# Two tiles' rows turned on TensorE in attention's last slot, and routing's steps moved by one place

## The chip, the cores and the metric

The kernel runs on one core of a Trainium2 chip. The metric is device time in microseconds (us) of one execution, the median of three runs. Engines are named as in the profile: PE is TensorE (PEld its weight load), DVE is VectorE, ACT is ScalarE, POOL is GpSimd, SP is SyncE, which here only issues DMAs.

## The reference

Inputs are q, k, v of shape (8, 8, 576, 64) (batch, heads, positions, head size), a gate matrix of 512x8, a local gate of 512x1, and for each of eight experts w1 (512x1024) and w2 (1024x512). What is computed, cut to what matters:

```python
scores = scale * np.matmul(q, k.transpose(0, 1, 3, 2))
scores = np.where(block_i >= block_j, scores, -1000000000.0)   # blocks of 64 positions
attn = np.exp(scores - max) / sum
x = np.matmul(attn, v)      # as (8, 576, 512)
...
logits = x @ w_gate
local_gate = 1.0 / (1.0 + np.exp(-(x @ w_local)))
for b in range(B):
    prev_e = -1
    for s in range(S):
        fresh_e = int(np.argmax(logits[b, s]))
        e = fresh_e if s == 0 or local_gate[b, s] < 0.5 else prev_e
        prev_e = e
        p = softmax(logits[b, s])
        out[b, s] = p[e] * (np.maximum(x[b, s] @ w1[e], 0.0) @ w2[e])
```

So each row of x goes to one expert, and which one may depend on the row before it in the same batch.

## The kernel before, in words

**Attention** runs in 32 slots, one for each pair of heads of a batch (loop at L1184; four slots make a batch). A slot i holds, in the order of the code: `behind(i)` (the values of pair i-1 on PE, L1007; sums and logits of a half batch, L705, with a copy on ACT, L714; four additions on DVE, L1019, in `add_chunks`), then the scores of pair i (L971 to L973) with the exponentials on ACT (L983, L995), then the transposes for pair i+1 (`kq`, L692, copied to `qkT` by ACT, L945), then `turns_of(i)` (x of an earlier batch is turned to rows by PE, `trx`, scaled by DVE, L818, and stored).

**Routing** is a generator of steps (`tokens`, L304 to L399; the class `Steps`, L16 to L59). A step ends in a `yield` of its kind: "V" for DVE alone, "T" or "PE" where the next step begins with a product on PE. The code of the slots calls for steps at fixed places, `steps.tensor()` for one that begins on PE, `steps.all()` for all that are left. Four steps of a group of batches begin on PE: `rta` (L329, a transpose; DVE reads it at L331 to L336), `rtb` (L339; read at L343 to L346), `rtd` (L349; read at L351, and L352 to L356 make the one-hot `oh` from it) and `rtr` (L362, L363: counts of `oh`; copied by DVE at L365 and L367). Then DVE goes on alone (L370 to L394), and the factors p[e] are stored by SP (L399, which the trace shows as L673 or L677). The third group (ten blocks of 128 rows) has its turn in slots 30 and 31, the last batch's later, between the expert tiles.

**The banks.** These products write to PSUM tiles of two banks, which `bank_of` (L894) gives out: a second taker gets the other half of the same tile, except that a name that begins with "rt" always begins a fresh tile. Waits go by tile: who writes into one half waits for readers of the other.

**Expert tiles.** Rows of one expert are gathered (POOL, L651) into tiles of 128 (`xgs`). A tile needs its rows with the 512 values on the partitions (`xT`), the expert's w1 as bf16 in a contiguous buffer (a DVE copy of 128x4096: L1071 for the first two tiles, L1337 for those that follow), the first products (`first_mm`, 32 on PE, L1086; ReLU on ACT, L1089), the second (`second_mm`, 8 on PE, L1283; scaled by ACT, L1291) and an indirect store by POOL (L1294). The expert of a tile is known only at run time: its number is loaded into registers of PE and DVE (L1095).

The rows of the first four tiles (`AHEAD`) are turned by four DMA transposes on SP's queue at the end of slot 30 (L1253), into `free`, a part of an attention buffer that is no longer used (shown as S); later tiles' rows by DMA transposes from the tile loop (L1350). The first tile's weights go to Pc of even pairs, after slot 31's `behind`; the second's to `qkT`, after pair 31's values; the third's to `w1c`, a buffer at the place of `qkT`.

**Handing over**, in the order of the code: slot 31; POOL's drain (L1261); values of pair 31 (L1007); a routing step that begins on PE (`rtr`); the second tile's weights (L1071); the last `add_chunks` (L1019); `steps.all()` (L1268: routing's L370 to L394); the first tile's products; the last half batch's gates (L705); then the tile loop, whose turn i brings weights of tile i+1, first products of tile i, steps of the last batch's routing (`point()`), gathers and second products of tile i-1. In turn i = 1 stand the second tile's first products. Steps of the last batch that the prediction speaks of: L705 to L710, the logits (`trl` on PE, L728; DVE at L737 to L753) and its own `tokens` (L312 to L394), with rows turned at L720.

Of the kernel before, what the change touches and what calls it, by code (L numbers as in the profile page):

```python
# [62 lines left out]
def kernel(  # L63
# [11 lines left out]
    nc = tc.nc  # L75
# [753 lines left out]
    with tc.tile_pool(name="atn_const", bufs=1) as cst, \  # L829
# [63 lines left out]

        def bank_of(nm):  # L894

            if not half or nm.startswith("rt"):
                half.clear()
                ps = psp.tile([P, 2, 512], F32, tag="sc", name=nm)
                half.extend([ps[:, 1], ps[:, 0]])
            return half.pop()  # L900
# [2 lines left out]
            half.clear()  # L903
            return psp.tile([P, 2, 512], F32, tag="sc", name=nm)

        half = []
        banks["of"], banks["both"] = bank_of, banks_of
        po = psp.tile([P, 1024], F32, tag="o", name="o", bufs=1)

# [121 lines left out]
        def turns_of(i):  # L1031

            b, r = divmod(i, HP)
            if r == 1 and b:
                return [lambda: logits_of(b - 1)]
            if r == 2 and b:
                return [lambda: rows_of_batch(b - 1, (0, 1)), lambda: rows_of_batch(b - 1, (4,))]
            if r == 3 and b:
                return [lambda: rows_of_batch(b - 1, (2, 3))]
            return []  # L1040

        T1 = scratch_of_weights(0)

# [102 lines left out]
        def run(tasks):  # L1146
            for task in tasks:
                half.clear()
                task()()
# [34 lines left out]
        for i in range(NPAIR):  # L1184
            slot[0] = i
            load_qk(i + 2)


            swap = i == 1
            if not swap:  # L1190
                behind(i)
            if i == NPAIR - 1:

                tiles = [(0, j) for j in range(NS[0])] + [(1, j) for j in range(NS[1])]
                ev = {j: expert(*tiles[j]) for j in range(2)}
                w = weights_at(bf(Pc[0], WE), ev[0])
            soon = 2 < i < NPAIR - 1 and i % 2
            if soon:
                last_scores(i)
            for u in range(len(UNITS)):  # L1200
                ps = scores(i, u)
                if u < 2 or i < 2:
                    exps(i, u, ps)
                if u == 0:
                    if not soon:
                        last_scores(i)
                    if i == 0:
                        transposes(1, 8)
                        constants()
                        for h in range(2):  # L1210
                            hs = slice(64 * h, 64 * h + 64)
                            nc.sync.dma_start(
                                out=wg2[hs, :, 16 * h:16 * h + E],
                                in_=moe_w_gate.rearrange("(p h d) e -> h d p e", h=2, d=D)[h])
                            nc.sync.dma_start(
                                out=wg2[hs, :, 16 * h + E:16 * h + E + 1],
                                in_=moe_w_local.rearrange("(p h d) e -> h d p e", h=2, d=D)[h])
            if swap:
                behind(i)
            last = lambda: exps(i, 2, ps) if i > 1 else None  # L1220
            if i == NPAIR - 2:
                last()
                last = lambda: None
                run([lambda: half_batch(B - 1, 0)])
            if i:
                transposes(i + 1, 6 if swap else 0,
                           last)
            if swap:
                add_chunks(i - 1)
            if i == NPAIR - 1:  # L1230
                routing(i)
            run(turns_of(i))
            slot[0] = i + 0.5
            if i % HP == 0 or NPAIR - 3 <= i < NPAIR - 1:
                routing(i)
            if i < NPAIR - 1:
                vector(END[i % HP])
            arrange(i + 2, [nc.gpsimd.tensor_copy] * 2)
            while pending:
                pending.pop(0)()  # L1240

            if wload < 2 * E - 2 and i == 2 + 2 * wload:
                load_weights(*divmod(wload, 2))
                wload += 1
            if i < NPAIR - 1:
                release(queue=nc.gpsimd)
            if i == NPAIR - 2:

                free = bf(Sb[(NPAIR - 3) % NSB], 2 * S * 2)[:, -AHEAD * Dm:]
                xTs = {}  # L1250
                for j in range(AHEAD):
                    xTs[j] = free[:, j * Dm:(j + 1) * Dm].rearrange("p (k n) -> p k n", k=KO1)
                    nc.sync.dma_start(out=xTs[j], in_=row_of_x(xgs[j]), transpose=True)  # L1253
                load_weights(E - 1, 1)
        assert not pending
        slot[0] = NPAIR
# [8 lines left out]
        steps.tensor()  # L1265
        w_next = weights_at(qkT.rearrange("p j a s -> p (j a s)").bitcast(BF16)[:, :WE], ev[1])
        add_chunks(NPAIR - 1)
        steps.all()  # L1268

        hT = op.tile([P, S], F32, tag="oT", name="hT", bufs=HP + 3)  # L1270
        prev = first_mm(xTs.pop(0), w, hT.bitcast(BF16)[:, :FO * P].rearrange("p (k n) -> p k n", k=FO),
# [3 lines left out]
    with tc.tile_pool(name="ffn_s", bufs=2, reuse_waits="tile") as f_p, \  # L1275
# [77 lines left out]

        def gathers(last, behind=None):
            while nx[0] <= min(last, len(tiles) - 1):
                if tiles[nx[0]] == (1, 0) and (chain.next, others.next) != ("end", "end"):
                    if nx[0] > i + 2:
                        break
                    others.all()
                    chain.all()  # L1360
                    release()
                gather(*tiles[nx[0]], behind=behind)

# [28 lines left out]
        for i, (ph, j) in enumerate(tiles):  # L1392
            now, done = w, prev
            waiting = len(held)
            if i == 0:
                w = w_next
            elif i + 1 < len(tiles):
                w = weights_of(i + 1)
            if i:

                prev = first_mm(xTs.pop(i), now, f_p.tile([P, FO, P], BF16, tag="hT", name="hT"), ps_h,
                                point if i > 1 else lambda: None)
            if i:
                point()

                gathers(i + AHEAD, relu[0] if i > NS[0] + 1 else None)


                second_mm(*tiles[i - 1], done, ev.pop(i - 1), factor_of(xgs[(i - 1) % NX]),
                          between=lambda: i < NS[0] + 1 and gathers(i + NX - 1))  # L1410
            else:
                gathers(NX - 1)
            if i + 2 >= AHEAD:
                rows_of(i + 2)

            release(waiting)
            if i:
                point()
            if i == behind_tile - 2:

                stay = nc.values_load(used[0:1, 1:2], engines=(mybir.EngineType.PE,),
                                      min_val=0, max_val=1)
                tc.mark_branch_hint_location("more", stay, engines=[mybir.EngineType.PE])
            if i == behind_tile:

                nc.gpsimd.drain()
                n = nc.values_load(used[0:1, 0:1], min_val=0, max_val=E * BS)
                with tc.If(n > NS[1] - MORE, label="more"):
                    more_tiles()
# [38 lines left out]
```

## Time and profile before

| | |
|---|---|
| median of three runs | 416.24 us (415.08 to 416.38) |
| the profiled execution | 414.38 us |
| its span in the profile | 412.6 us |
| mean granted clock of PE | 0.997 |
| PE busy | 394.3 us (96%), 5762 matmuls |
| PEld busy | 282.9 us (69%) |
| DVE busy | 245.8 us (60%), 511 instructions |
| ACT busy | 239.7 us (58%), 415 instructions |
| POOL busy | 192.3 us (47%), 224 instructions |
| last attention values end, first expert products begin | 263.4 us |
| last matmul ends | 407.6 us |

The profile comes from one execution. Its span is that part in which the hardware profiler saw instructions, and the time of the execution is 1.8 us more. Start times count from the span's start. A row of the timeline names start, busy time, engine, line, operation and tiles ("o<-S,v" is a product that writes o from S and v); a bracket behind it gives the idle time of that engine before it and what is taken to have ended it. Rows of one line that follow each other closely are one row with a count, and matmuls overlap, so that sums of their durations are more than the time in which they ran.

### The profile page before, as it was taken

The numbers are of one execution on the slowest core, as the hardware profiler recorded it, in microseconds if no ns is written. First come the engines' busy times: TensorE is split into PE (matmuls) and PEld (weight loads), VectorE is DVE, ScalarE is ACT, GpSimd is POOL, SyncE is SP. The second block draws the span as 40 slices with busy tenths as digits, with TensorE's granted clock in tenths as the row PEclk, the third lists the DMA queues.
The fourth block names the chain that finished last, engine by engine and source line by source line (L and its number), as shares of the span: only waits on it lengthen the run. The fifth ranks groups of instructions, "written<-read, shape, count | busy, mean of one in ns | idle before, by whom it ended". The sixth has DMA issues, their size and how long they took to land.

```text
span 412.6 us, 14349 instructions
## 1 busy us (share of the span) xinstructions
PE 394.3 (96%) x5762; PEld 282.9 (69%) x5762; DVE 245.8 (60%) x511; ACT 239.7 (58%) x415; POOL 192.3 (47%) x224
## 2 busy tenths in 40 slices
PE   8999999999999999999999799799999999999995
PEld 7676767667667667767766566567777777777763
DVE  3453574674574476985899985887887333333320
ACT  3768557657657756766675555434545555555542
POOL 1225341451253141671632325046775888888833
PEclk9999999999999999999999999999999999999998
DMA  6579999999989979999899589946563665555452
GB/s 175 138 169 194 174 209 224 172 208 238 191 197 226 192 180 224 181 186 225 156 213 188 150 143 203 164 106 132 145 165 112 159 140 154 144 147 151 128 99 79
DMA packets 108819, 69.97 MB, mean 170 GB/s; under 512 B 74847, under 2 KB 100255, under 8 KB 108752
## 3 DMA queue, kind: packets, MB, share of 16 engines
q0 software_dynamic: 19200, 34.84, 41.5%
q1 hardware_dynamic: 89552, 34.19, 38.6%
q8 instruction: 48, 0.79, 0.8%
q14 instruction: 19, 0.16, 0.1%
HBM read 66.88 MB, written 14.70 MB: 198 GB/s over the span
## 4 chain that ended last, share of the span: by engine, by line
PE 77%; DMA 10%; ACT 7%; issue 2%; DVE 2%; SPq 1%; POOL 1%; POOLq 0%; DVEq 0%; ACTq 0%
PE o L1007 20%; PE ps_h L1086 15%; PE ps_y L1283 14%; PE sc L973 13%; PE trg L705 6%; ACT Pc L983 4%; DMA xg<-x_rows,idx 3%; DMA qkl<-in_q_dram 3%; PE kq L692 2%; DMA v<-in_v_dram 2%; DMA x_rows<-xg 2%; PE trx L692 1%; ACT S L983 1%; PE o L692 1%; PE o L993 1%
## 5 line engine op out<-in xcount | busy, mean ns | idle before, releaser
L1019 DVE TENSOR_TENSOR S<-S,Pc 128x896 f32<-128x896 f32 (+3 forms) x128 | 96.8, 756 | 23.7 <-PE o L1007 16.3
L878 POOL COPY w_bf<-w_bf 128x512 f32<-128x512 f32 x61 | 45.8, 763 | 109.0 <-DMA w_bf<-in_k_dram 53.4
L973 PE MATMUL sc<-qkT 64*64 64x224 f32 (+6 forms) x1536 | 90.3, 366 | 0.0
L1337 DVE COPY w1c<-w_bf 128x4096 bf16 x36 | 44.3, 1231 | 55.3 <-PE ps_h L1086 53.1
L1086 PEld LDWEIGHTS <-w1c 128*128 128x128 bf16 x1152 | 67.3, 98 | 9.1 <-issue 2.0
L1283 PE MATMUL ps_y<-w_bf,hT 128*128 x304 | 71.7, 379 | 0.0
L973 PEld LDWEIGHTS sc<-qkT 64*64 64x64 f32 x1536 | 64.9, 133 | 4.7
L1086 PE MATMUL ps_h<-xT,w1c 128*128 128x128 bf16 x1088 | 66.3, 219 | 1.3 <-PEq L1095 1.0
L983 ACT ACTIVATE Pc<-sc 128x448 f32<-128x448 f32 (+1 forms) x96 | 66.7, 710 | 0.0
L1294 POOL DMA_INDIRECT out_dram<-y,idx x38 | 55.8, 1468 | 23.1 <-issue 9.5
L651 POOL DMA_INDIRECT xg<-x_rows,idx x38 | 47.2, 1243 | 35.7 <-issue 17.8
L1089 ACT ACTIVATE hT<-ps_h 128x512 bf16<-128x512 f32 x76 | 45.3, 597 | 26.2 <-PE ps_h L1086 22.7
L1007 PE MATMUL o<-Pc,v 128*64 128x320 f32 (+2 forms) x512 | 57.3, 366 | 0.0
L1011 ACT COPY oT<-o 128x576 f32<-128x576 f32 x32 | 20.4, 639 | 56.5 <-PE o L1007 56.5
L1291 ACT ACTIVATE y<-ps_y,xg 128x512 f32<-128x512 f32 (+1 forms) x38 | 25.9, 681 | 46.5 <-PE ps_y L1283 40.7
L1007 PEld LDWEIGHTS o<-Pc,v 128*64 128x64 f32 x512 | 34.6, 137 | 24.1
L983 ACT ACTIVATE S<-sc 128x576 f32<-128x576 f32 x64 | 41.8, 653 | 16.0 <-PE sc L973 10.9
L1283 PEld LDWEIGHTS <-hT 128*128 128x128 bf16 x304 | 28.2, 98 | 27.7 <-issue 0.5
L1007 PE MATMUL o<-S,v 128*64 128x256 f32 (+1 forms) x256 | 38.1, 418 | 0.8 <-ACT qkT L924 0.6
L677 POOL DMA_DIRECT2D x_rows<-xg x31 | 17.1, 555 | 40.7 <-DVE xg L818 37.2
L945 ACT COPY qkT<-kq 128x1024 f32<-128x1024 f32 x30 | 30.9, 1029 | 0.2 <-PE kq L692 0.2
L818 DVE TENSOR_TENSOR xg<-trx,rs 128x512 bf16<-128x512 f32 (+1 forms) x31 | 19.7, 682 | 15.5 <-PE trx L692 15.4
(304 smaller groups left out, 404.7 us busy)
## 6 DMA issues: line engine op xcount, KB each, us to landing
w_bf<-in_moe_w_dram POOLq DMA_DIRECT2D x16, 1024.0 KB, 11.5
w_bf<-in_k_dram SPq DMA_DIRECT2D x32, 256.0 KB
w_bf<-in_q_dram SPq DMA_DIRECT2D x32, 256.0 KB
v<-in_v_dram SPq DMA_DIRECT2D x64, 128.0 KB
x_rows<-xg POOLq DMA_DIRECT2D x24, 128.0 KB, 5.8
qkl<-in_k_dram SPq DMA_DIRECT2D x32, 32.0 KB
qkl<-in_q_dram SPq DMA_DIRECT2D x32, 32.0 KB
vl<-in_v_dram SPq DMA_DIRECT2D x32, 32.0 KB
```

The lines of the kernel that those rows point to most:

```text
L651: st = nc.gpsimd.indirect_dma_start(out=x, out_offset=None, in_=x_dram[:rows], in_offset=bass.IndirectOffsetOnAxis(ap=row_of(ph, j), axis= ...
L878: copies[j](m, raws[i][1 + j].rearrange("p h j d -> p j h d"))
L945: nc.scalar.copy(to.rearrange("p a (r s) -> p r a s", r=2), ps.rearrange("p r (a s) -> p r a s", a=2))
L973: nc.tensor.matmul(to[:, col + skip:col + n], lhsT=t[r, 0, k0:k0 + ST], rhs=t[r, 1, q0 + skip:q0 + n], start=True, stop=True)
L983: nc.scalar.activation(exps_at(i, c, q0, n, rows), ps[rows, :, col:col + n], func=AF.Exp, scale=scale_attn)
L1007: nc.tensor.matmul(po[64 * h:64 * h + 64, VO + q0:VO + q0 + n], lhsT=vv, rhs=exps_at(i, c, q0, n, slice(0, P))[:, h, :], start=(c == 0), s ...
L1019: nc.vector.tensor_add(Ss[i][rows, :, P * c:], Ss[i][rows, :, P * c:], Pc[i % 2][rows, :, POS[c]:POS[c] + n])
L1086: nc.tensor.matmul(ps[:, fo, :], lhsT=w[:, ko * F + f0:ko * F + f0 + P], rhs=xT[:, ko, :], start=(ko == 0), stop=(ko == KO1 - 1))
L1089: relu[0] = nc.scalar.activation(hT[:, half * (FO // 2):(half + 1) * (FO // 2), :], ps, func=AF.Relu)
L1283: nc.tensor.matmul(ps, lhsT=hT[:, fo, :], rhs=w2_bf[:, bass.ds(ev + fo * Dm, Dm)], start=(fo == 0), stop=(fo == FO - 1))
L1294: st = nc.gpsimd.indirect_dma_start(out=out_flat, out_offset=bass.IndirectOffsetOnAxis(ap=row_of(ph, j), axis=0), in_=y, in_offset=None, b ...
L1337: ended["w"] = nc.vector.tensor_copy(w, w1_bf[:, bass.ds(ev[i], WE)])
```

## The change

Line numbers behind L895 grow by 12 to 20 in the new kernel: L1019 becomes L1019 still, L1071 becomes L1083, L1086 becomes L1098, L1095 becomes L1107, L1253 becomes L1270, L1283 becomes L1299, L1337 becomes L1353 and L1350 becomes L1366.

- In slot 30 a routing step that begins on PE is taken right behind the half batch's products. While `shared[0]` is set, an "rt" name takes the other half of a tile, so this step (`rta`) writes into the half batch's tile. Each of the four steps then comes one place earlier: `rtb` at the end of slot 30, `rtd` behind pair 30's values, `rtr` at the end of slot 31's scores.
- In slot 31, behind that step, `rows_ahead()` turns the rows of the first two tiles on PE, eight transposes of 128x128 bf16 into the other half of `rtr`'s tile, and ACT copies the 128x1024 to `free`. DMA transposes are left for the third and fourth tile.
- `steps.all()` stands in turn 1 of the tile loop, behind the third tile's weights, and no longer ahead of the loop. Turn 1 has no `point()` after its first products.
- `release()` (held DMA issues) is called ahead of the first tile of the second phase in every case.

```diff
-            if not half or nm.startswith("rt"):
+            if not half or nm.startswith("rt") and not shared[0]:
...
-        half = []
+        half, shared = [], [False]
...
+        ON_CHIP = 2
+
+        def rows_ahead():
+
+            ps = bank("xT").bitcast(BF16)
+            for j in range(ON_CHIP):
+                for ko in range(KO1):
+                    o = (KO1 * j + ko) * P
+                    nc.tensor.transpose(ps[:, o:o + P], row_of_x(xgs[j])[:, ko * P:(ko + 1) * P],
+                                        id_b)
+            nc.scalar.copy(free[:, :ON_CHIP * Dm], ps)
...
                 run([lambda: half_batch(B - 1, 0)])
+                shared[0] = True
+                steps.tensor()
+                shared[0] = False
...
             if i == NPAIR - 1:
                 routing(i)
+                rows_ahead()
...
                 for j in range(AHEAD):
                     xTs[j] = free[:, j * Dm:(j + 1) * Dm].rearrange("p (k n) -> p k n", k=KO1)
-                    nc.sync.dma_start(out=xTs[j], in_=row_of_x(xgs[j]), transpose=True)
+                    if j >= ON_CHIP:
+                        nc.sync.dma_start(out=xTs[j], in_=row_of_x(xgs[j]), transpose=True)
...
         add_chunks(NPAIR - 1)
-        steps.all()
...
-                if tiles[nx[0]] == (1, 0) and (chain.next, others.next) != ("end", "end"):
-                    if nx[0] > i + 2:
-                        break
-                    others.all()
-                    chain.all()
+                if tiles[nx[0]] == (1, 0):
+                    if (chain.next, others.next) != ("end", "end"):
+                        if nx[0] > i + 2:
+                            break
+                        others.all()
+                        chain.all()
                     release()
...
                 w = weights_of(i + 1)
+                if i == 1:
+                    steps.all()
...
             if i:
-                point()
+                if i > 1:
+                    point()
```

In the new kernel's program, the instructions of DVE around the handing over stand in this order (left out are the sizes; "x4" counts instructions): L331, L333, L336, L818 x3, L343, L345, L346, L351, L352, L354, L356, L1019 x4 (pair 30), register loads (L1107), L1083 (first tile's weights), L365, L367, L818 x2, L1083 (second tile's weights), L1019 x4 (pair 31), L1353 (third tile's weights), L370 to L394, L710, L1353 (the fourth's). In the old one L351 to L356 and L818 x2 stand behind the first tile's weights, and L370 to L394 ahead of the third tile's.

## The prediction

> **What bounds the kernel now.** I read the page's span first, then the table of stretches, then TensorE's timeline where attention hands over to the expert tiles.
>
> ```profile
> span 412.6 us, 14349 instructions
> ```
> ```profile
> 264.00:270.00 6.00, 3.59 (x61) 2.96 (x59) 5.54 (x15) 2.12 (x5) 0.37 (x1) 1.00 1.13 121
> 284.00:394.00 110.00, 110.00 (x1255) 80.49 (x1252) 55.52 (x96) 57.06 (x92) 85.40 (x61) 1.00 0.58 143
> 407.60:410.10 2.50, 0.00 (x0) 0.00 (x0) 0.48 (x1) 0.47 (x1) 1.32 (x2) 1.00 0.38 146
> 410.10:412.60 2.50, 0.00 (x0) 0.00 (x0) 0.00 (x0) 0.00 (x0) 0.00 (x0) 0.50 0.14 53
> ```
>
> Columns: stretch, its length, busy time (instructions) of TensorE (PE), weight load, VectorE (DVE), ScalarE (ACT) and GpSimd; then the granted TensorE clock, DMA share, GB/s. From 284 to 394 TensorE is busy for 110.00 of 110.00 us. So nothing later can swallow a delay: what the change does to the moment at which TensorE reaches 284 is what it does to the end. The whole change lies between 250 and 284.
>
> ```profile
> 252.76 0.27 PE L329 MATMUL rta<-id_f,lt_g 128*10 128x128 f32 x1 [0.44 <-ACT qkT L945]
> ...
> 255.82 0.20 PE L339 MATMUL rtb<-lt_g,ones_f 10*10 10x10 f32 x2
> ...
> 258.92 0.23 PE L349 MATMUL rtd<-id_f,ltmp_g 10*128 10x10 f32 x1
> 259.86 0.71 PE L692 MATMUL trx<-id_f,oT 64*128 64x64 f32 x16 [0.71 <-ACT Pc L983]
> ...
> 263.44 1.95 PE L1086 MATMUL ps_h<-S,Pc 128*128 128x128 bf16 x32
> 265.32 0.75 PE L705 MATMUL rtr<-oT,wg 128*32 128x320 f32 x8
> 268.47 1.95 PE L1086 MATMUL ps_h<-S,qkT 128*128 128x128 bf16 x32 [2.41 <-DVE S L1019]
> 270.35 1.28 PE L705 MATMUL trg<-S,sel 128*32 128x320 f32 x16
> 271.56 1.90 PE L1283 MATMUL ps_y<-w_bf,hT 128*128 x8
> ```
>
> A line is start, busy time, engine, line of the kernel, output and inputs; the bracket is idle time before it and who is taken to have ended it. TensorE stands 2.41 us before the second tile's first product (268.47).
>
> **What that wait is.** The view names an addition on DVE (L1019), but those additions write pair 31's scores, which these products do not read. They read the second tile's transposed rows, in another of the S buffers, and the weights in qkT.
>
> ```profile
> 250.38 12.27 SPq L1253 DMA_TRANSPOSE S<-xg  x4
> ```
> ```profile
> 256.63 2.92 DVE L1019 TENSOR_TENSOR S<-S,Pc 128x896 f32<-128x896 f32 x4
> 260.86 1.23 DVE L1071 COPY Pc<-w_bf 128x4096 bf16 x1 [1.31 <-issue]
> 262.01 0.16 DVE L351 CAST lt_g<-rtd 128x10 int32<-128x10 f32 x1
> ...
> 262.62 0.24 DVE L356 TENSOR_TENSOR oh<-w,pay 128x80 bf16<-128x80 f32 x1
> 262.78 1.28 DVE L818 TENSOR_TENSOR x<-trx,rs 128x512 bf16<-128x512 f32 x2
> 263.98 0.23 DVE L365 COPY lt_g<-rtr 128x80 f32<-128x80 f32 x1
> 264.12 0.23 DVE L367 COPY ltmp_g<-rtr 128x80 f32<-128x80 f32 x1
> 264.27 1.22 DVE L1071 COPY qkT<-w_bf 128x4096 bf16 x1
> ```
>
> The weights were there at 264.27 + 1.22 = 265.49. The four DMA transposes occupy SP's queue from 250.38 to 262.65, so what came last is a transpose. The change takes this one off the DMA, and the wait goes: **-2.4** (the 2.41 of the bracket).
>
> **Step by step.** I follow how late TensorE is against the run before.
>
> *Slot 30.* L329 now writes into half_batch's tile, so it waits until ACT has copied that tile out.
>
> ```profile
> 250.93 0.43 ACT L714 COPY LT<-trg 128x320 f32<-128x320 f32 x1 [0.39 <-PE trg L705]
> ```
>
> The copy begins as the products end, at 250.93. In the old order TensorE goes on to other transposes; in the new one it stands until the copy is done and seen, about 251.4 (0.5), and then transposes (about 0.2, as its 0.27 overlaps what follows). Behind it in TensorE's queue are the next slot's transposes (L692), and behind these ACT's qkT copy and the values. The place that L329 leaves is taken by rtb (L339), beneath the 0.44 us wait for qkT, which stays. **+0.7.** DVE's part (L331 to L336) lies beneath those transposes.
>
> *Slot 31: the new wait.* The eight transposes (L1050) go into the other half of rtr's tile. The tile is guarded as one, so the first of them waits until DVE has read rtr: for L367. DVE takes its instructions in order, and in the new order L367 stands behind this row: L351 to L356, the four additions of pair 30, the expert's register loads (the 1.31 us of "issue"), the first tile's weights, L365. The row starts when rtd does, now straight after pair 30's values. rtb followed those at 255.82; without it and with the delay rtd comes at 256.55 and ends at 256.8. Then 262.62 + 0.24 - 262.01 = 0.85 for L351 to L356, 2.92, 1.31, 262.01 - 260.86 = 1.15 for the weights, and 264.12 + 0.23 - 263.98 = 0.37: 6.60 in all, so 263.4. TensorE is through with the scores at 258.92 before (rtd follows); with +0.7, rtd's 0.23 ahead of them instead of rtb's 0.20, and rtr's two small products, it is there at 259.7. **It waits 3.7 us.** Queued behind it are trx, pair 31's values and tile 0's products: the path itself.
>
> The eight transposes are not in the trace. The nearest rows are bf16 matmuls of the same size, 16 in 0.89 us, and float transposes, four in 0.45 (fence below): 0.45 to 0.9 for eight, and I take 0.45, the row of the same type. trx then begins at 263.4 + 0.45 = 263.85 instead of 259.86: +4.0, in which the +0.7, rtd's leaving and trx's own 0.71 wait are contained. rtr's two products no longer stand ahead of tile 0 (-0.15): **+3.85**.
>
> [...]
>
> ACT's copy of 128x1024 (L1052) is 1.4 us at most, by the 0.43 of the 128x320 one (0.43 x 3.2). It lies beneath pair 31's values, which take 2.87 us (from trx's end at 260.57 to 263.44), and would cost those 1.4 if tile 0's products followed at once. The other two tiles' DMA transposes move up in SP's queue with two ahead of them gone; they are first read at about 275. SP has less to do and nothing waits for it.
>
> *Tile 1.* 3.85 - 2.4 = **+1.45** at the start of tile 1's products; their weights are there at about 267.1 (263.85 + trx 0.71 + L818 1.28 + 1.22), and TensorE at 266.07 + 3.85 = 269.9.
>
> *The third tile's weights and routing.* The weights go into the buffer that holds qkT, so they wait for the end of tile 1's products as before, in either order: nothing is gained. But routing's 14 instructions (L370 to L394), which lay mostly in that stall, now stand behind them, ahead of L710 and the next copies.
>
> ```profile
> 268.40:273.42 5.02, 4.29 (x16) 1.00 0.32 77
> 275.00:278.70 3.70, 3.31 (x14) 1.00 0.73 177
> ```
> ```profile
> 274.54 0.66 PE trl L728 x6
> 275.20 0.89 PE ps_h L1086 x16
> 276.09 1.73 PE ps_y L1283 x8
> 277.82 0.89 PE ps_h L1086 x16
> 278.71 0.45 PE trx L720 x4
> 279.15 0.89 PE ps_h L1086 x16
> 280.05 0.11 PE rta L329
> 280.16 1.73 PE ps_y L1283 x8
> 281.88 0.14 PE rtb L339 x2
> 282.02 0.30 issue
> ```
>
> The first fence is DVE alone (routing, third weights and L710; then L737 to L326), the second the chain of waits. From the end of tile 1's products DVE now has 5.02 + 3.70 and two further weight copies of 1.15 before rta's input (L326): 11.0 us, or by busy time alone 4.29 + 3.31 + 2.30 = 9.9. TensorE gets to rta after two ps_y at 1.73, trg 1.28, four halves of ps_h at 0.89, trl 0.66 and trx 0.45: 9.4. It waits 0.5 to 1.6 there. The 0.44 of rtb and "issue" at the end of the chain falls into that wait: 0 to +1.15. I take **+0.6**, nearer the elapsed than the busy time. routing's stores of the factors (SP) go out later with it, and the first of the later tiles' row transposes, which stood behind them in SP's queue, now goes ahead of them. The chain of waits names neither up to 282, and I cost this at nothing; a row that came late would hold up its tile as it did the second one here. GpSimd's gathers wait for ACT's y, as before.
>
> Sum without the clock: 1.45 + 0.6 = **+2.05**.
>
> *The clock.* In the two rows at the end of the first table TensorE is idle from 407.60; the clock is 1.00 for 2.5 us and then 0.50. In 264 to 270, with its gap of 2.41, it stays 1.00. If one length of idleness decides, these rows put it between 2.4 and 2.5 us, and the new wait of 3.7 is over it, with only rtr's two products in it. What half speed costs is not shown, as the kernel ends in it: at least nothing, at most half of a wait's length, 1.85. I take half of the 2.5 us for which the trace shows it: **+1.25**. Sum: **+3.3**.
>
> [...]
>
> The profiled execution took 414.38 us, 1.8 more than its span; the median of the runs is 416.24. The sum is made in the profiled one (414.38 + 3.3 = 417.7) and added to the median: **419.5**.
>
> **The rivals.**
>
> 1. *The clock stays.* Same waits, full speed: 416.24 + 2.05 = 418.3. For it: only one gap is over the limit, and by little. Chance 0.27.
> 2. *The register loads run early.* If DVE's loads no longer cost 1.31 in the new order, the wait is 2.4, the length at which the clock held: 2.05 - 1.3 = +0.75, 417.0. Against it: the loads stand in DVE's own queue behind the additions, as before. Chance 0.05.
> 3. *Faster: no wait in slot 31.* If DVE gets to L367 as soon as rtr is there, the transposes start at about 260.5 (rtr, L365, L367), 2.9 earlier, and DVE is ahead enough that the 0.6 goes too: 2.05 - 2.9 - 0.6 = -1.45, 414.8. It decides only if L367 is done by about 260.7. Against it is DVE's order: 2.92 + 1.31 + 1.15 must come first. Chance 0.06.
> 4. *Dearer transposes.* One after another at L329's 0.27 they cost 2.16, 1.7 more than in the forecast: 421.2. Chance 0.07.
> 5. *The old wait stays*, because L1019 really ends it: then TensorE, at 270, meets additions that end at about 270.4, so 0.4 remains. That is inside the range, and within the chance of the forecast.
>
> **How the numbers follow.** The forecast (both waits, clock halved) has 0.55. The range takes in rival 1 with the second wait at nothing (418.3 - 0.6, and 0.3 for the spread of the runs: 417.4) and the forecast with the clock at 1.85 and transposes at 0.9 (420.55, with the same 0.3 and rounded up: 421.0). It holds 0.55 + 0.27 = 0.82. About 0.3%, 1.25 us, is what a measurement of this kernel can tell from no change: faster 0.06 (rival 3), within 0.05 (rival 2), slower 0.89.
>
> **What would show it.** In the profile after: a wait of 3 to 4 us before the first L1050, ended by DVE (L367); no wait worth naming before tile 1's products; about 1 us before batch 7's L329; a clock under 1.00 in the 4 us behind the new wait; TensorE again without a gap from some 286 on. The forecast is wrong if L367 runs ahead of the additions of pair 30, if the wait ends near 261, or if the old 2.4 us stands again before tile 1.

## The result

The changed kernel takes 419.49 us (median of 21 runs, 416.24 to 424.39), the one before 415.49 us in the 21 runs beside it (413.61 to 418.78). The ratio is 1.0074, 95% interval 1.0053 to 1.0094: slower by 3.1 us of 416. It is an estimate of its own and not the quotient of the medians, which are 4.0 us apart, and it leaves out slow executions (one of these 21, one of e4's four below, one of the kernel before on chip B). The profiled execution took 418.33 us, span 416.4. The forecast was 419.5, range 417.4 to 421.0.

**The profile after.** First TensorE's timeline of the changed kernel, around the handing over (columns as in the prediction):

```profile
250.22 0.75 PE L705 MATMUL trg<-oT,wg 128*32 128x320 f32 x8
...
252.83 0.27 PE L329 MATMUL trg<-id_f,lt_g 128*10 128x128 f32 x1 [0.52 <-ACT LT L714]
...
261.04 0.21 PE L362 MATMUL rtr<-oh,upper 128*128 128x80 bf16 x1
...
264.38 0.61 PE L1050 MATMUL rtr<-id_b,xg 128*128 128x128 bf16 x8 [3.10 <-DVE ltmp_g L367]
264.92 0.71 PE L692 MATMUL trx<-id_f,oT 64*128 64x64 f32 x16
...
268.42 1.96 PE L1098 MATMUL ps_h<-S,Pc 128*128 128x128 bf16 x32
270.31 0.75 PE L705 MATMUL trg<-oT,wg 128*32 128x320 f32 x8
270.99 1.96 PE L1098 MATMUL ps_h<-S,qkT 128*128 128x128 bf16 x32
...
278.17 0.27 PE L728 MATMUL trl<-id_f,LTl 128*64 128x128 f32 x1
...
284.12 0.27 PE L329 MATMUL rta<-id_f,S 128*5 128x128 f32 x1 [1.71 <-DVE S L326]
...
407.83 3.62 PE L1299 MATMUL ps_y<-w_bf,hT 128*128 x16
```

The 2.41 us ahead of the second tile's products (270.99) are gone. In their place stand 0.52 (L329), 3.10 (the first L1050) and 1.71 us (batch 7's L329). Two rows of the kernel before give the places to count from:

```profile
248.79 0.74 PE L705 MATMUL trg<-oT,wg 128*32 128x320 f32 x8
...
403.97 3.62 PE L1283 MATMUL ps_y<-w_bf,hT 128*128 x16
```

Slot 30's half batch begins 1.43 us later in the changed kernel's profile (250.22 against 248.79), before anything that the change touches; that is the start of one execution against another. From there to the last sixteen products it is 155.18 us before and 157.61 after: **+2.43 us** is what the change costs in this pair of profiles.

DVE's timeline, changed kernel: the row of work that ends the 3.10 us, then that which ends the 1.71 (routing's L370 to L394 lie between 274.18 and 277.28).

```profile
258.85 0.24 DVE L356 TENSOR_TENSOR oh<-w,pay 128x80 bf16<-128x80 f32 x1
259.00 2.86 DVE L1019 TENSOR_TENSOR S<-S,Pc 128x896 f32<-128x896 f32 x4
262.81 1.23 DVE L1083 COPY Pc<-w_bf 128x4096 bf16 x1 [0.94 <-DVE S L1019]
263.95 0.23 DVE L365 COPY lt_g<-rtr 128x80 f32<-128x80 f32 x1
264.10 0.23 DVE L367 COPY ltmp_g<-rtr 128x80 f32<-128x80 f32 x1
...
272.99 1.23 DVE L1353 COPY w1c<-w_bf 128x4096 bf16 x1 [2.05 <-PE ps_h L1098]
...
277.69 1.37 DVE L1353 COPY w1c<-w_bf 128x4096 bf16 x1
278.99 0.34 DVE L737 RECIPROCAL rs<-trl 128x32 f32<-128x32 f32 x1
...
281.51 0.20 DVE L314 TENSOR_TENSOR S<-L,S 128x40 f32<-128x40 f32 x1
282.00 1.23 DVE L1353 COPY w1c<-w_bf 128x4096 bf16 x1 [0.29 <-issue]
283.15 0.20 DVE L317 SCALAR_TENSOR_TENSOR S<-S,w 128x40 f32<-128x40 f32 x1
```

rtr is ready for DVE at 261.3, and DVE gets to it at 263.95: four additions, the register loads (0.94 us) and the first tile's weights come first. Further down DVE has no idle time from the third tile's weights (272.99) to 281.71; the fifth tile's weights (282.00) stand in the middle of rta's input, between L314 and L317. L737, the first reader of trl, begins at 278.99 as a copy of weights ends, while trl was done at 278.44: here it is DVE's own queue, routing in it, that is late.

The clock in this profile, the wait and the stretch behind it (PE, PEld, DVE, ACT, POOL busy; PEclk; DMA share; GB/s):

```profile
261.00:264.50 3.50, 0.40 (x7) 0.27 (x6) 2.35 (x5) 1.84 (x3) 0.00 (x0) 1.00 1.19 181
264.50:268.00 3.50, 3.50 (x46) 2.44 (x46) 2.33 (x3) 1.01 (x1) 0.00 (x0) 1.00 1.24 195
```

It stays at 1.00: the sign that the forecast named, a clock under 1.00 in the 4 us behind the wait, is not in this profile. Each run records the mean clock over its span, the idle end included (0.997 in the profile of the kernel before, whose clock fell only at the end). Half speed over the whole 5.0 us behind the kernel before's last matmul would give 0.994 (an estimate: half of 5.0 us off 412.6). Over the 21 runs of the changed kernel the median is 0.992, and in 13 of them it is 0.993 or less: there, by this estimate, the clock fell elsewhere too, though these runs do not show where.

### The profile page after: what moved, and what is told of

It reads as the page before. It is cut to its first block, busy times and chain, and to the rows that moved or that the text cites. A ratio compares the mean times of both kernels' runs of the same rounds, so it can differ in the third digit from the quotient of the medians.

```text
span 416.4 us, 14361 instructions
## 1 busy us (share of the span) xinstructions
PE 396.9 (95%) x5770; PEld 284.4 (68%) x5770; DVE 246.0 (59%) x511; ACT 241.1 (58%) x416; POOL 194.1 (47%) x224
## 4 chain that ended last, share of the span: by engine, by line
PE 77%; ACT 7%; DVE 7%; DMA 4%; issue 3%; POOL 1%; POOLq 0%; DVEq 0%; ACTq 0%
PE o L1007 21%; PE sc L973 15%; PE ps_h L1098 13%; PE ps_y L1299 12%; PE trg L705 6%; DMA xg<-x_rows,idx 4%; ACT Pc L983 4%; PE kq L692 3%; DVE S L1019 2%; ACT S L983 2%; PE o L692 1%; PE trx L692 1%; PE idle L1119 1%; PE o L993 1%; DVE w1c L1353 1%
## 5 line engine op out<-in xcount | busy, mean ns | idle before, releaser
L1019 DVE TENSOR_TENSOR S<-S,Pc 128x896 f32<-128x896 f32 (+3 forms) x128 | 97.1, 758 | 23.1 <-PE o L1007 17.1
L878 POOL COPY w_bf<-w_bf 128x512 f32<-128x512 f32 x61 | 48.1, 803 | 103.3 <-DMA w_bf<-in_k_dram 60.0
L973 PE MATMUL sc<-qkT 64*64 64x224 f32 (+6 forms) x1536 | 91.4, 368 | 0.0
L1353 DVE COPY w1c<-w_bf 128x4096 bf16 x36 | 44.4, 1232 | 56.9 <-PE ps_h L1098 54.5
L1098 PEld LDWEIGHTS <-w1c 128*128 128x128 bf16 x1152 | 67.3, 98 | 9.5 <-DVE w1c L1353 1.7
L1299 PE MATMUL ps_y<-w_bf,hT 128*128 x304 | 71.7, 379 | 0.0
L1098 PE MATMUL ps_h<-xT,w1c 128*128 128x128 bf16 x1088 | 67.0, 219 | 0.9 <-ACTq L1448 0.8
L1310 POOL DMA_INDIRECT out_dram<-y,idx x38 | 57.1, 1501 | 22.4 <-issue 10.4
L651 POOL DMA_INDIRECT xg<-x_rows,idx x38 | 45.3, 1193 | 38.6 <-ACT y L1307 19.3
L1299 PEld LDWEIGHTS <-hT 128*128 128x128 bf16 x304 | 28.2, 98 | 27.2
L818 DVE TENSOR_TENSOR xg<-trx,rs 128x512 bf16<-128x512 f32 (+1 forms) x31 | 19.7, 682 | 16.7 <-PE trx L692 16.5
```

Source lines behind the costliest of these rows:

```text
L651: st = nc.gpsimd.indirect_dma_start(out=x, out_offset=None, in_=x_dram[:rows], in_offset=bass.IndirectOffsetOnAxis(ap=row_of(ph, j), axis= ...
L878: copies[j](m, raws[i][1 + j].rearrange("p h j d -> p j h d"))
L973: nc.tensor.matmul(to[:, col + skip:col + n], lhsT=t[r, 0, k0:k0 + ST], rhs=t[r, 1, q0 + skip:q0 + n], start=True, stop=True)
L1019: nc.vector.tensor_add(Ss[i][rows, :, P * c:], Ss[i][rows, :, P * c:], Pc[i % 2][rows, :, POS[c]:POS[c] + n])
L1098: nc.tensor.matmul(ps[:, fo, :], lhsT=w[:, ko * F + f0:ko * F + f0 + P], rhs=xT[:, ko, :], start=(ko == 0), stop=(ko == KO1 - 1))
L1299: nc.tensor.matmul(ps, lhsT=hT[:, fo, :], rhs=w2_bf[:, bass.ds(ev + fo * Dm, Dm)], start=(fo == 0), stop=(fo == FO - 1))
```

## The experiments

They ran on three chips (A: e1 to e4; B: e5 to e8; C: e9 to e12). On A and B the kernel before took longer (median 419.99 and 418.93) than on C (415.67), so times are compared on one chip only. Line numbers of the experiments differ by a few from the changed kernel's. The wait columns are TensorE's, from each profile.

| run | median us (runs) | ratio to before, 95% | median of mean clocks | wait before L1050 | wait before batch 7's rta |
|---|---|---|---|---|---|
| e1 before again | 420.99 (10) | 1.0035 (0.9994 to 1.0075) | 0.994 | none | 0 |
| e2 filler | 422.17 (10) | 1.0049 (1.0013 to 1.0086) | 0.996 | 1.35 | 1.69 |
| e3 first weights later | 423.70 (10) | 1.0082 (1.0039 to 1.0125) | 0.993 | 1.21 | 1.27 |
| e4 routing back | 427.22 (4) | 1.0112 (1.0007 to 1.0218) | 0.988 | 3.45 | 1.70 |
| e5 point back | 423.26 (4) | 1.0103 (1.0056 to 1.0150) | 0.991 | 3.25 | 0 |
| e6 tail back | 424.10 (4) | 1.0114 (1.0060 to 1.0169) | 0.984 | 3.25 | 0 |
| e7 early steps only | 418.39 (10) | 0.9991 (0.9962 to 1.0021) | 0.994 | none | 0 |
| e8 e3 and e6 together | 419.24 (12) | 1.0015 (0.9986 to 1.0044) | 0.993 | 1.21 | 0 |
| e9 changed again | 419.00 (10) | 1.0081 (1.0051 to 1.0112) | 0.992 | 3.26 | 1.72 |
| e10 filler again | 416.22 (10) | 1.0025 (0.9987 to 1.0062) | 0.997 | 1.36 | 1.72 |
| e11 rows alone | 415.02 (12) | 0.9986 (0.9955 to 1.0017) | 0.998 | none | 0 |
| e12 rows, third weights | 414.95 (12) | 0.9994 (0.9963 to 1.0025) | 0.999 | none | 0 |

### What the wait before L1050 is: e3

```diff
-                ev = {j: expert(*tiles[j]) for j in range(2)}
-                w = weights_at(bf(Pc[0], WE), ev[0])
...
                 rows_ahead()
+                ev = {j: expert(*tiles[j]) for j in range(2)}
+                w = weights_at(bf(Pc[0], WE), ev[0])
```

> The changed kernel with the first tile's weight copy and the register loads ahead of it (L1083, L1107) placed behind L365 and L367 in DVE's order, and nothing else. Theory (the wait before L1050 is DVE's order, not the transposes or the bank): L367 ends about 2.0 us earlier, the wait falls from 3.10 to about 1.1, tile 0's weights are still in time (264.5 against 266.4), and everything later on TensorE, the wait before rta of 1.71 included, moves up by 2.0: -2.0 from the changed kernel, ratio to before about 1.002. Rival (the wait is the price of the transposes themselves or of the PSUM bank): the transposes start at the same distance from rtr and the ratio stays 1.007.

TensorE's timeline of e3:

```profile
262.97 0.21 PE L362 MATMUL rtr<-oh,upper 128*128 128x80 bf16 x1
...
264.43 0.61 PE L1050 MATMUL rtr<-id_b,xg 128*128 128x128 bf16 x8 [1.21 <-DVE ltmp_g L367]
265.57 0.71 PE L692 MATMUL trx<-id_f,oT 64*128 64x64 f32 x16 [0.53 <-PE rtr L1050]
```

From rtr to the transposes it is 1.46 us instead of 3.34: one copy and its loads moved, the wait is 1.9 shorter. So it is DVE's order. trx gains only 1.3 of that: it now waits 0.53 itself, put down to L1050; for what is not shown. The time did not follow: 1.0082, against the 1.002 expected. A clock drop stands in its profile well before the change (0.50 from 231.39 to 234.80), and on this chip the kernel before spreads over 417.5 to 423.3; what this edit alone is worth in time is not shown.

### What the wait before rta is: e4, e5, e6

e4 puts routing (L370 to L394) back ahead of the tile loop:

```diff
         add_chunks(NPAIR - 1)
+        steps.all()
...
-                if i == 1:
-                    steps.all()
```

> The changed kernel with steps.all() back ahead of the tile loop, so that L370 to L394 stand before the third tile's weights in DVE's order. Theory (the 1.71 us wait before batch 7's rta is DVE's queue, which the moved routing filled): the routing lies in DVE's idle 2.05 us before the third weights, which come 1.1 us later and still before TensorE needs them; the wait before rta falls from 1.71 to 0 to 0.7: -1.0 to -1.7, ratio to before 1.003 to 1.005. Rival (the third weights being early is worth something): TensorE waits before the third tile's products by as much, no change of the ratio of 1.0074.

The wait before rta stays, 1.70 us. DVE's timeline of e4:

```profile
281.75 0.49 DVE L710 TENSOR_TENSOR LTl<-LTl,trg 128x320 f32<-128x320 f32 x1 [1.81 <-PE trg L705]
282.25 1.23 DVE L1354 COPY w1c<-w_bf 128x4096 bf16 x1
284.50 0.36 DVE L737 RECIPROCAL rs<-trl 128x32 f32<-128x32 f32 x1 [1.02 <-PE trl L728]
```

DVE itself is idle here, 1.81 for trg and 1.02 for trl, which TensorE now makes behind the third tile's products. So routing's 3.1 us alone are not what makes rta late: with them gone, trl comes last, at nearly the same moment (L737 begins 7.79 us behind the second tile's first product, 276.71, against 8.00 in the changed kernel). e5 leaves routing where the change put it, and restores the point():

```diff
-                if i > 1:
-                    point()
+                point()
```

> The changed kernel with the point() after tile 1's first products restored; routing still stands behind the third tile's weights. With it the last batch's logits (trl) come half a tile earlier and the fourth tile's weight copy no longer stands between L314 and L317 in DVE's order. Theory 1, of the prediction (routing's 3.1 us in DVE's queue make the 1.71 us wait before rta): the wait stays, 1 us or more, before rta. Theory 2 (the missing point makes it: the weight copy in the middle of rta's input and too few products between trl and rta): no wait before rta; trl, now earlier, waits 0.5 to 1.0 for L710 instead.

TensorE's timeline of e5:

```profile
281.74 0.44 PE L728 MATMUL trl<-id_f,LTl 128*128 128x128 f32 x2 [0.62 <-DVE LTl L710]
...
287.08 0.27 PE L329 MATMUL rta<-id_f,S 128*5 128x128 f32 x1
...
289.89 0.19 PE L339 MATMUL rtb<-S,ones_f 5*5 5x5 f32 x2 [0.82 <-DVE S L336]
290.64 1.95 PE L1098 MATMUL ps_h<-xT,w1c 128*128 128x128 bf16 x32 [0.56 <-PE rtb L339]
```

No wait before rta, as theory 2 has it: the missing point() had moved trl behind the third tile's products and brought the fifth tile's weight copy between L314 and L317. But the time is not won. With point() back, the late routing holds up TensorE at other places: trl waits 0.62 for L710, rtb 0.82, and the products behind it 0.56. e6 is both edits together.

> The changed kernel with both the point() and steps.all() where they stood before; what is left of the change is slots 30 and 31. By both theories no wait before rta nor before trl, and the chain from tile 1's products to rta is that of the kernel before; 1.7 us less than the changed kernel, some 0.7 us more than the kernel before in a profile without clock drops (ratio about 1.002). If a wait of over 0.5 us stands at the third tile's products, putting the third tile's weights ahead of routing was worth that much.

Neither wait is there, and none ahead of the third tile's products. What each is worth shows from the second tile's first product to the seventh's, a stretch with the same work on TensorE and the clock at 1.00 in all five:

| | second tile (qkT) | seventh tile | between |
|---|---|---|---|
| kernel before | 268.47 | 290.13 | 21.66 |
| changed kernel | 270.99 | 293.95 | 22.96 |
| e4, routing back | 276.71 | 299.65 | 22.94 |
| e5, point() back | 274.99 | 298.45 | 23.46 |
| e6, both back | 274.70 | 296.21 | 21.51 |

So either of the two, routing behind the third tile's weights or the missing point(), is enough for a loss of 1.3 to 1.8 us, and only both together take it away. The time of e6 is far over the expectation (1.0114 instead of 1.002), and so is that of e4 (1.0112 instead of 1.003 to 1.005); e5 took 1.0103. Their clocks are a part of the reason.

### The clock: e4 to e6, e1, e2, e9, e10

Stretches of e6, then of the kernel before run again (e1):

```profile
262.00:264.50 2.50, 0.00 (x1) 0.00 (x0) 1.53 (x3) 1.55 (x3) 0.00 (x0) 1.00 1.23 197
264.50:271.50 7.00, 6.25 (x44) 4.03 (x45) 4.74 (x8) 1.01 (x1) 2.28 (x2) 0.51 0.52 103
```
```profile
268.00:271.00 3.00, 0.29 (x8) 0.10 (x1) 2.71 (x5) 0.68 (x2) 0.00 (x0) 1.00 1.35 156
271.00:274.50 3.50, 3.41 (x32) 3.27 (x31) 2.60 (x13) 0.60 (x1) 2.02 (x2) 0.51 0.27 78
```

In e6 the clock falls inside the wait and stays at half for 6.83 us, twice the 3.41 us of e1; e4 and e5 show the same (0.54 from 266.0 to 273.5, 0.51 from 264.5 to 271.5). From rtr to the end of tile 0's products e6 takes 261.75 to 274.02, 12.27 us, where the changed kernel's profile takes 9.27 with a wait shorter by 0.15: the fall costs 2.85 (2.66 and 2.54 by the same count in e4 and e5). In e1, the kernel before, the old wait (2.80 us there) is followed by these 3.41 us at half speed (271.01 to 274.42). So a fall could follow the old wait too. Nor are these the only ones: e6 has two more, at 254 and 404, and e1 one at 230.

> The kernel before, run again for the mean clock of each of its runs. If the changed kernel's extra time beyond its waits comes from clock drops that the new wait sets off, the runs here have a mean clock of about 0.996 to 1.000 (one drop at most, at the end), against 0.985 to 1.000 with a median of 0.992 for the changed kernel. If the drops come from elsewhere (attention, the start), the clocks here spread as widely as those of the changed kernel. Time 1.000 of before either way.

Median 0.994, 0.989 to 0.995: not the narrow band of the first branch. The drops are not the changed kernel's alone. To see what the new wait adds, e2 and e10 fill it with work that changes nothing else:

```diff
-        ON_CHIP = 2
+        ON_CHIP, FILL = 2, 8
...
+            for j in range(FILL):
+                nc.tensor.matmul(po[:, VO:VO + P], lhsT=zeros, rhs=zeros, start=True, stop=True)
             ps = bank("xT").bitcast(BF16)
```

> The changed kernel with eight products of zeros (each some 0.33 us by the row of four records in 0.71 us at the start of the run before) put between rtr and the first L1050, so that TensorE has work for about 2.6 of the 3.10 us in which it waits for L367. The zeros' result is written over by the values. The wait's end is DVE's, so the profile's times stay (transposes at 264.4, from the half batch's products on +0.0 to +0.3). Theory that the wait sets off clock drops: the mean clocks rise to those of the kernel before and the time falls by 1 to 2 us, ratio to before about 1.003. Rival, drops come from elsewhere: clocks and ratio (1.0074) as for the changed kernel.

On chip A: ratio 1.0049 and mean clocks of 0.995 or more in all ten runs, but with no run of the changed kernel beside it. So both ran together on chip C:

> The changed kernel again, beside the runs below on one chip. In three of the four profiles so far that hold the whole wait before L1050 (3.10 to 3.45 us) the granted clock fell to 0.5 within the wait and stayed there for about two windows of 3.4 us. Theory that the wait sets this off in most runs: median of the mean clocks 0.985 to 0.992, ratio to before 1.007 to 1.011. Rival (the drops were chance): mean clocks as before's, median 0.995 or more, ratio 1.006.

> The changed kernel with the eight products of zeros in the wait, beside it on one chip. Theory: without the gap no drop there; median of the mean clocks 0.995 to 0.997, time 1 to 3 us under the changed kernel's, though no wait is shorter. Rival (the drops are chance, or come from elsewhere): clocks and times of the changed kernel.

TensorE's timeline of e9, then of e10:

```profile
260.44 0.21 PE L362 MATMUL rtr<-oh,upper 128*128 128x80 bf16 x1
...
263.94 0.61 PE L1050 MATMUL rtr<-id_b,xg 128*128 128x128 bf16 x8 [3.26 <-DVE ltmp_g L367]
```
```profile
259.04 0.21 PE L362 MATMUL rtr<-oh,upper 128*128 128x80 bf16 x1
259.08 0.21 PE L363 MATMUL rtr<-oh,ones_b 128*128 128x80 bf16 x1
259.12 2.03 PE L1047 MATMUL o<-const-float32-0.0 128*128 128x128 f32 x16
262.51 0.61 PE L1052 MATMUL rtr<-id_b,xg 128*128 128x128 bf16 x8 [1.36 <-DVE ltmp_g L367]
```

The transposes begin 3.50 and 3.47 us behind rtr: no wait of DVE is shorter, TensorE merely has 2.03 us of empty work. The median falls from 419.00 to 416.22, the ratio from 1.0081 (1.0051 to 1.0112) to 1.0025 (0.9987 to 1.0062), and runs with a mean clock of 0.993 or less from 7 of 10 to 1 of 10. Among the 35 runs of the kernel before on that chip they are 14. So filling the wait gains, and fewer falls of the clock go with it. That the clock is all of the 2.8 us is not shown. Among the runs with a mean clock of 0.995 or more the mean times are 418.2 for e9 (only 3 runs), 416.5 for e10 (8) and 415.4 for the kernel before (19), so 1.8 lies between runs of much the same clock. e9's own profile, like the first one, shows no fall behind the wait, and its execution still took 2.6 us more than that of e10's profile: 1.4 of this lies ahead of slot 30's half batch, 0.9 in a wait for a row by DMA at 328.18, and next to none in the waits of the change.

### Whether the old wait was DMA's: e7

The change without `rows_ahead()`: four DMA transposes again, point() and steps.all() where they were.

> The kernel before with routing's four steps moved up one place only: no transposes on TensorE, four by DMA, steps.all() and point() where they were. Theory (the move costs 0.7 in slot 30, and the wait before tile 1's products is ended by a DMA transpose, whenever TensorE gets there): L329 waits about 0.5 for ACT's copy, the wait before tile 1's products stays and is shorter by about what TensorE is late, 1.5 to 2.4 us, and the time is that of before within 0.3 us. Rival (that wait is ended by DVE's L1019, as the view names it): it follows DVE's additions, which follow pair 31's values, and so it moves with TensorE and stays at 2.4, time +0.7.

TensorE's timeline of e7, then DVE's:

```profile
267.97 0.74 PE L705 MATMUL trg<-oT,wg 128*32 128x320 f32 x8
268.96 1.95 PE L1098 MATMUL ps_h<-S,qkT 128*128 128x128 bf16 x32 [0.25 <-PE trg L705]
```
```profile
267.47 2.93 DVE L1019 TENSOR_TENSOR S<-S,Pc 128x896 f32<-128x896 f32 x4
```

The additions run until 270.40, the second tile's products begin at 268.96: L1019 does not hold them up, though the view of the kernel before names it. The transposes on SP's queue do fit: the products begin 17.4 us behind the first of them in e7 (251.53), 18.1 in the kernel before (250.38), 17.6 in e1 (253.48). The rival's 2.4 is out; my 1.5 to 2.4 too, since TensorE came later here (L329 waited 1.50, and the clock fell at 254). The time, 0.9991, is as expected. But the old wait has a successor: further down TensorE's timeline of e7 has one that the kernel before has not:

```profile
275.19 1.07 PE L1098 MATMUL ps_h<-S,w1c 128*128 128x128 bf16 x16 [1.23 <-DVE w1c L1352]
```

In DVE's order the third tile's weights come behind routing, and routing behind the additions.

### Versions meant to keep the gain: e8, e11, e12

e8 is e3 and e6 in one.

> The changed kernel with the first tile's weight copy behind L367, and with point() and steps.all() where they stood before. Theory: the wait before L1050 is 1.2 (as measured with that copy moved alone), trx follows after about 0.5, no wait before rta: the changed kernel's +2.4 in its profile less 1.3 less 1.7 is -0.6 from the kernel before, ratio 0.998 to 1.000. If the waits have other causes than DVE's order and the missing point, it stays above 1.004.

It came out at 1.0015 (0.9986 to 1.0044), slightly over: the waits are as expected (1.21 before L1050, 0.68 before trx, none before rta), but L329 in slot 30 waits 1.66, where the sum of the expectation has the 0.52 of the changed kernel's profile. Its stretch from the second to the seventh tile is 21.71 us, as in the kernel before. From there to the last sixteen products it takes 2.3 us more than the kernel before's profile (116.12 against 113.84), in part in waits of 1.2 us together (a row by DMA, "issue") between 324 and 331; e1, the kernel before itself, takes 3.5 more there, so that this is not put down to the edit.

e11 starts from the kernel before, turns the rows on TensorE, behind trx, with a bank pair of their own, and puts the first tile's weights behind them:

```diff
             run(turns_of(i))
+            if i == NPAIR - 1:
+                rows_ahead()
+                ev = {j: expert(*tiles[j]) for j in range(2)}
+                w = weights_at(bf(Pc[0], WE), ev[0])
```

> The kernel before with the rows of the first two tiles turned on TensorE behind trx, in a tile of their own, and the first tile's weight copy behind that in DVE's order; routing's steps and steps.all() stay. The transposes wait for L351 at most, no wait of over 0.3 us there. Theory: +0.5 for the transposes, the 2.4 us wait before tile 1 goes, but routing's 3.1 us, which lay in it, now hold up the third tile's weights by about 1.3: -0.6 against before, ratio 0.997 to 1.000. Rival (the wait before tile 1 comes back in another form): ratio 1.001 or more.

TensorE's timeline of e11:

```profile
259.94 0.71 PE L692 MATMUL trx<-id_f,oT 64*128 64x64 f32 x16 [0.71 <-ACT Pc L983]
260.58 0.62 PE L1051 MATMUL xT<-id_b,xg 128*128 128x128 bf16 x8
...
273.75 1.05 PE L1099 MATMUL ps_h<-S,w1c 128*128 128x128 bf16 x16 [1.95 <-DVE w1c L1353]
```

The transposes follow trx without a wait, and the old one is gone. But 1.95 us stand ahead of the third tile's products: routing, which had run inside the old wait, now holds up their weights. The gain is given back in the next wait: from slot 30's half batch to the last sixteen products it is 155.15 us (249.06 to 404.21) against 155.18, and the ratio 0.9986 (0.9955 to 1.0017).

> As the run with the rows alone, but with the third tile's weights ahead of routing, point() kept. Theory: no wait before the third tile's products; trl waits 0.6 to 0.9 for L710 and rtb up to 0.8 instead, as in the run with point() restored: -0.5 to -1.0 against before, ratio 0.997 to 0.999, about that of the rows alone. If putting these weights first was the useful part of the change, it is faster than the rows alone by over 0.5 us.

With the third weights first it is 0.9994 (0.9963 to 1.0025): trl waits 0.70, rtb 0.61 and the products behind it 0.54 instead. No version here is shown to be faster than the kernel before.

## Why the prediction was right, and where it was not

- **Slot 30, +0.7: right.** The wait is 0.52, ended by L714, which reads the tile's other half. From the half batch to pair 30's values it is 4.17 us before (248.79 to 252.96) and 4.89 after (250.22 to 255.11). On chips A and B the same wait was 1.5 to 1.7; there ACT came to its copy later (in e6 3.39 us behind the half batch's first product, 248.17 to 251.56, against 2.13 in the changed kernel, 250.22 to 252.35).
- **The wait before L1050, 3.7: right in place and cause, 0.6 too long.** 3.10 and 3.26, ended by L367, which reads the other half of rtr's tile. The register loads took 0.94, not 1.31. e3 shows the cause, DVE's order.
- **Transposes, 0.45 to 0.9: 0.61** as a group, trx follows 0.54 behind their start. The 0.27 apiece of rival 4 is out.
- **trx +4.0, tile 0 +3.85, tile 1 +1.45**: measured from the half batch +3.63, +3.55, +1.09.
- **The old wait goes, -2.4: right.** That DMA and not DVE ended it was argued from the code; e7 shows that it was not L1019 and is in keeping with the DMA, and in e11, where the rows no longer come by DMA, the wait is gone.
- **The wait before rta, +0.6 for "routing's 14 instructions ... ahead of L710 and the next copies": half of the cause, and a term too small.** The wait is 1.71, and from tile 1 on the loss grows from 1.09 to 2.43, +1.34. The sum by elapsed time was right: DVE takes 10.98 us from the third tile's weights to the end of L326 (272.99 to 283.97), where I had 11.0. I then went halfway to the sum of busy times, 9.9, which leaves out the gaps between the instructions. What I did not have is that the point() left out is a second cause, of the same size: it moves trl behind the third tile's products, so that without routing DVE waits for trl instead (e4). With point() back, routing alone costs 1.80 (e5: 23.46 against 21.66), with routing back, the missing point() alone 1.28 (e4).
- **The later tiles' rows, nothing: right in the first profile,** where no such wait stands. In e9's there is one of 0.92 at 328.18, in e7's, with all four early transposes left on the DMA, one of 1.63 at 327.11; whether the change has a part in them is open.
- **Sum without the clock +2.05: +2.43** in the profile; by the same count 2.22 in e10's (248.33 to 405.73), and 3.30 in e9's (249.76 to 408.24), with the row at 328 in it.
- **The clock, +1.25: not seen where it was forecast, and wrong in size and in what it is set against.** In both profiles of the changed kernel the clock stays at 1.00 behind the wait, which is rival 1. In e4 to e6, with the same wait, it falls, and costs 2.54 to 2.85, not 1.25, and more than the 1.85 that I took for the most. The kernel before has falls of its own, one behind its old wait (e1), where I had counted none. Filling the wait takes 2.8 us off the median (e9, e10), of which the clock's share is open. Against the kernel before, what is left for the clock and all else is 3.1 - 2.4 = 0.7 us of the measured ratio.
- **The total, 419.5 against 419.49: luck to the tenth.** The forecast adds 3.3 to a median of 416.24; the kernel before then had 415.49, so that the medians lie 4.0 apart, and 3.1 by the ratio. In the sum the waits were 0.4 too small and the clock too large. What was right is the side, the size of some 3 us, and that most of it is the two waits.
- **The limit "between 2.4 and 2.5 us" of idleness: wrong.** 3.10 and 3.26 us left the clock at 1.00 in two profiles, behind 2.80 it fell in another, and so it did behind waits of 1.50 to 2.09 (last section).

## What to carry to other kernels

When a transfer is replaced by work on an engine, look at which tile the result goes into, who else reads that tile, and what stands ahead of that reader in its own engine's order: here four additions, register loads and a weight copy, 5.0 us together (259.00 to 263.95), ahead of two reads of 0.2 us turned a gain of 2.4 us into a loss of 1.1 at the second tile. A wait that disappears was also cover for what ran inside it (routing's 3.1 us), and a step left out of a written order shifts everything that its neighbours wait for. Where two moves can each make the same engine late, taking back one of them proves little: measure the whole stretch and not only the wait that went. If the bounding engine gets a gap of some 2 to 3 us, count its clock as well, with a chance and not as a certainty, and count the same for the gap that goes: here it went to half within waits of 3.25 to 3.45 us (e4 to e6) and at the end of one of 2.80 (e1), and stayed at 1.00 through 3.10 and 3.26 (the changed kernel's two profiles).

## What the runs showed of the hardware that was not expected

The clock's half-speed stretches ahead of the last matmul last 3.41 to 3.42 us (nine in e1 to e7) or twice that (e4 to e6 behind the wait, 6.83 us). Behind the wait they begin inside the gap: in e4 to e6 the clock fell 1.9 to 2.6 us into the wait behind rtr (at 266.38, 264.54 and 264.56), 0.7 to 1.3 us before the transposes. Within one profile the falls lie whole multiples of one length apart, 3.413 us (e1's 40.96 / 12), to 0.03 us: in e1 at 230.05, 271.01 and 417.78 (12 and 43 lengths), in e6 at 254.32, 264.56, 404.51 and 421.58 (3, 41 and 5), and so in e2 to e5 and e7. That is the length of the short stretches.

If this spacing holds all through a profile (an estimate from these falls), the moments at which the clock could fall can be counted back in steps of 3.413 us from any fall, the one at the kernel's end too. In the changed kernel's two profiles, where the clock held, such a moment would cut the wait in two: 3.10 us into 1.5 and 1.6 (at 262.75, counted from 416.34), 3.26 into 1.8 and 1.4 (at 262.50, from 416.09). In e1 and e4 to e6, where it fell, 1.9 to 2.7 us of the wait lie ahead of the fall. By this estimate it would be where a wait lies on these steps that counts, and not its length alone; shown is that the clock fell at the end of 2.80 us (e1) and held through 3.26 us (e9). How much of a step would have to be idle is not shown: in e5 a wait of 2.34 us at 404.13 to 406.47, 2.0 of it in one step, left the clock at 1.00. On chips A and B falls at 230 to 231, 254 to 256 and 404 to 406 us, in seven of the eight profiles there, came 1.0 to 2.3 us behind waits of 1.50 to 2.09 us, while in other profiles such waits left the clock at 1.00 (1.66 us before L329 in e8, 1.97 us from 228.49 on in the changed kernel's).
